# SSM convolution and SwiGLU on one core: kernel transforms split by even and odd samples, mirrored rows fetched by index, residual added by matmul

One NeuronCore of one Trainium2 chip. The metric is the device time of one launch in microseconds (us). Short names of the engines: PE (TensorE), PEld (its weight loads), DVE (VectorE), ACT (ScalarE), POOL (GpSimd), SP (SyncE).

## The reference

For a sequence of 2048 rows of 640 columns in bf16: a causal shift convolution of four taps on k, a product with v, a long causal convolution with an SSM kernel (one filter of 2048 taps for each column), a skip term, a product with LayerNorm(q), a residual, then LayerNorm and a SwiGLU FFN of width 1728 with its residual.

```python
def _A_ref(q, k, v, shift_k, ssm_k, ssm_D):
    # k_shift = causal 4-tap convolution of k (cut)
    kv = k_shift * v
    # y = irfft(rfft(kv padded to 2S) * rfft(ssm_k padded to 2S))[:S]  (cut)
    y = y + kv * ssm_D[None, None, :]
    return q * y

def _B_ref(x, w_gate, w_up, w_down):
    return (silu(x @ w_gate) * (x @ w_up)) @ w_down

x = A_q
h = x + _A_ref(_layernorm(x), A_k, A_v, A_shift_k, A_ssm_k, A_ssm_D)
return h + _B_ref(_layernorm(h), B_w_gate, B_w_up, B_w_down)
```

## The kernel before

The sequence is cut into four blocks of 512 rows. Each block of kv and of the SSM kernel is transformed by matmuls with cosine and sine tables (X and G below). Spectra are multiplied and summed on VectorE (`pair`), one inverse transform per block goes back, and LayerNorm, up and down projection follow. While VectorE works on the products of block n, PE does the FFN of block n-1. Every instruction is first entered in a plan with a duration, its reads and its writes. A small list scheduler in the kernel then fixes the order of each engine, and the engines run in that order.

The transform of an SSM kernel block, 8 output tiles from 4 contraction tiles of 512 samples:

```python
def g_transform(p, pr):
    for ct in range(NCT):                       # 8
        for kt in range(4):
            for h in range(2):
                nc.tensor.matmul(ps(g)[:, h, 0:NH], WG[:, kt, ct * P:(ct + 1) * P],
                                 gT[p][:, kt, h * NH:(h + 1) * NH], start=(kt == 0), stop=(kt == 3))
        # ScalarE copies PSUM to G[p] (cut)

def hbuild(p, pr):                              # for p = 1, 2, 3
    vop(TA, d[0][:], g[0][:], gp[1][:], ...)    # 2560 wide
    vop(TS, d[1][:], g[1][:], gp[0][:], ...)
```

The four-tap convolution of a 128-row tile of blocks 1 to 3, on VectorE:

```python
nc.vector.tensor_mul(kd[:], kd[:], w4[:])                            # 2560 wide
nc.vector.tensor_add(kd[:, 0:2, :], kd[:, 0:2, :], kd[:, 2:4, :])    # 1280 wide
nc.vector.tensor_add(kd[:, 0, :], kd[:, 0, :], kd[:, 1, :])
nc.vector.tensor_mul(kv[:, q, :], kd[:, 0, :], vb[:])
```

The end of a LayerNorm, on POOL, with one number per row. VectorE then scales the tile with it (tiles `xln` and `hl`):

```python
def fin():                                      # s is 128 x 8 float32
    e.tensor_scalar(s[:, 3:4], s[:, 1:2], 1.0 if vec else 1.0 / D, EPS, op0=ALU.mult, op1=ALU.add)
    e.tensor_tensor(s[:, 4:5], s[:, 3:4], mhalf[:], op=ALU.pow)   # e = nc.gpsimd
add("POOL", 1.5, fin, ...)
```

The inverse transform gives an even and an odd part of a half block. Their sum is one tile of y, and their difference is another tile with its rows reversed. Before, four matmuls with a flip matrix turn that one round, and VectorE multiplies from PSUM. The FFN's residual is a VectorE addition from PSUM.

## Time and profile before

| | before |
|---|---|
| device time, median of 3 | 296.56 us (294.88 to 296.61) |
| span of the profiled run | 293.2 us |
| busy PE / DVE / ACT / POOL | 275.7 / 229.7 / 169.7 / 65.7 us |
| VectorE ends the last spectrum product | 225.0 us |
| first up projection starts | 74.8 us |
| mean granted TensorE clock | 0.999 |

The span is that of the profiled execution; timed executions are some 2 us longer. A busy time is the union of the engine's instructions, so it is time covered, not work done.

### The profile page before, as it was taken

What the parts mean: (1) busy time and instruction counts of PE and PEld (TensorE: products, weight loads), DVE (VectorE), ACT (ScalarE), POOL (GpSimd) and SP (SyncE); (2) the same over time, 40 slices, a digit from 0 to 9 for tenths busy, and PEclk for the clock granted to TensorE, in tenths of its full rate; (3) what the DMA queues carried; (4) which work ended last, traced back from release to release, by engine and by line L of the source; (5) the groups of instructions that cost most, each with busy time, mean ns of one, the idle gap of its engine ahead of it and who ended that gap; (6) DMA issues with size and microseconds to landing.
All of it is one profiled execution on the core that took longest, in us unless ns stands there. A gap on an engine that the chain in (4) does not pass through costs nothing.

```text
span 293.2 us, 4406 instructions
## 1 busy us (share of the span) xinstructions
PE 275.7 (94%) x1651; PEld 157.8 (54%) x1651; DVE 229.7 (78%) x301; ACT 169.7 (58%) x323; POOL 65.7 (22%) x70
## 2 busy tenths in 40 slices
PE   3889969999999989999999999999999999999995
PEld 1567647667544535665546456555445664444563
DVE  0849797999999999999999999999999931211211
ACT  5136985897846499006986780269955822555300
POOL 0000371474000064000362193009800220000000
PEclk9999999999999999999999999999999999999999
DMA  7990699219454777925668293173653151654011
GB/s 246 386 353 2 173 269 335 54 27 301 135 137 107 205 208 155 294 108 139 161 202 233 61 194 68 45 207 86 168 128 99 49 119 54 172 146 102 0 47 46
DMA packets 67898, 44.13 MB, mean 151 GB/s; under 512 B 25442, under 2 KB 65955, under 8 KB 67748
## 3 DMA queue, kind: packets, MB, share of 16 engines
q1 hardware_dynamic: 66240, 40.23, 50.0%
q10 hardware_dynamic: 1636, 3.61, 3.3%
q8 instruction: 13, 0.21, 0.3%
q14 instruction: 9, 0.07, 0.1%
HBM read 37.28 MB, written 2.62 MB: 136 GB/s over the span
## 4 chain that ended last, share of the span: by engine, by line
DVE 53%; PE 31%; issue 5%; ACT 4%; DMA 3%; POOL 2%; ACTq 1%; SPq 0%
DVE s L453 20%; DVE T L453 14%; PE psF L644 11%; PE psF L618 11%; DVE k L378 3%; DVE tT L632 3%; PE psA L405 3%; DMA wu<-in_B_w_up_dram 2%; PE psF L361 2%; DVE k L379 2%; PE psA L550 2%; PE psA L443 2%; DVE k L380 1%; DVE o L652 1%; DMA wg<-in_B_w_gate_dram 1%
## 5 line engine op out<-in xcount | busy, mean ns | idle before, releaser
L618 PE MATMUL psF<-hT,wg 128*128 128x512 bf16 x280 | 69.4, 379 | 0.8 <-ACT uc L630 0.8
L524 POOL TENSOR_SCALAR sm<-sm 128x1 f32<-128x1 f32 x32 | 30.2, 943 | 168.4 <-ACT junk L521 157.9
L618 PE MATMUL psF<-hT,wu 128*128 128x512 bf16 x260 | 64.5, 379 | 0.9 <-DMA wu<-in_B_w_up_dram 0.9
L644 PE MATMUL psF<-wd,tT 128*128 128x320 bf16 x448 | 64.8, 300 | 0.5 <-DVE tT L632 0.4
L623 ACT ACTIVATE sg<-psF 128x512 bf16<-128x512 f32 (+1 forms) x56 | 33.8, 603 | 45.0 <-PE psF L618 36.0
L644 PEld LDWEIGHTS <-tT 128*128 128x128 bf16 x448 | 41.3, 97 | 23.6 <-issue 6.9
L453 DVE TENSOR_TENSOR T<-s,s 128x2560 bf16<-128x2560 bf16 x32 | 47.2, 1480 | 0.0
L453 DVE TENSOR_TENSOR s<-s,T 128x2560 bf16<-128x2560 bf16 x32 | 47.0, 1480 | 0.0
L618 PEld LDWEIGHTS <-wg 128*128 128x128 bf16 x280 | 27.2, 98 | 32.7 <-issue 2.3
L630 ACT CAST uc<-psF 128x512 bf16<-128x512 f32 (+1 forms) x56 | 33.2, 593 | 16.4 <-PE psF L618 16.2
L632 DVE TENSOR_TENSOR tT<-sg,uc 128x512 bf16<-128x512 bf16 (+1 forms) x56 | 23.2, 418 | 24.3 <-ACT uc L630 24.3
L618 PEld LDWEIGHTS <-wu 128*128 128x128 bf16 x260 | 25.3, 98 | 30.2 <-DMA wu<-in_B_w_up_dram 1.4
L525 POOL TENSOR_TENSOR sm<-sm,mhalf 128x1 f32<-128x1 f32 x32 | 35.1, 1098 | 2.7
L361 PEld LDWEIGHTS <-s 128*128 128x128 bf16 x256 | 25.0, 97 | 11.8 <-issue 2.1
L361 PE MATMUL psF<-wd,s 128*128 128x320 bf16 x192 | 28.4, 299 | 0.9 <-ACT wd L338 0.5
L652 DVE TENSOR_TENSOR o<-psF,x 128x640 bf16<-128x640 f32 x16 | 13.0, 815 | 19.3 <-PE psF L644 19.3
L364 ACT CAST s<-psF 128x640 bf16<-128x640 f32 x32 | 21.8, 693 | 7.7 <-PE psF L361 7.6
L521 ACT ACTIVATE junk<-x,sm 128x640 bf16<-128x640 bf16 x28 | 23.7, 847 | 0.3
L520 ACT ACTIVATE junk<-x 128x640 bf16<-128x640 bf16 x28 | 20.9, 747 | 3.8 <-DVE x L578 2.9
L550 PE MATMUL psA<-s,WI 128*128 128x320 bf16 x128 | 18.9, 299 | 2.7 <-DVE s L453 2.7
L453 DVE TENSOR_TENSOR s<-s,s 128x2560 bf16<-128x2560 bf16 x14 | 20.5, 1480 | 1.2 <-ACT s L364 1.2
L443 PE MATMUL psA<-kv,WX 128*128 128x320 bf16 x128 | 20.5, 299 | 0.0
(55 smaller groups left out, 232.0 us busy)
## 6 DMA issues: line engine op xcount, KB each, us to landing
k<-in_A_k_dram SPq DMA_DIRECT2D x12, 640.0 KB, 4.9
wg<-in_B_w_gate_dram SPq DMA_DIRECT2D x24, 320.0 KB, 3.2
wu<-in_B_w_up_dram SPq DMA_DIRECT2D x24, 320.0 KB, 3.7
out_dram<-o SPq DMA_DIRECT2D x16, 160.0 KB, 2.0
wd<-in_B_w_down_dram SPq DMA_DIRECT2D x1, 2080.0 KB, 10.7
v<-in_A_v_dram SPq DMA_DIRECT2D x12, 160.0 KB, 5.2
x<-in_A_q_dram SPq DMA_DIRECT2D x3, 640.0 KB, 5.5
tT<-in_A_ssm_k_dram SPq DMA_DIRECT2D x2, 640.0 KB, 8.8
```

The costliest lines, as they stand in the source:

```text
L361: nc.tensor.matmul(ps(g)[:, h, 0:NH], WG[:, kt, ct * P:(ct + 1) * P], gT[p][:, kt, h * NH:(h + 1) * NH], start=(kt == 0), stop=(kt == 3))
L443: nc.tensor.matmul(ps(g)[:, h, 0:NH], WX[:, kt, ct * P:(ct + 1) * P], kv[:, base + kt, h * NH:(h + 1) * NH], start=(kt == 0), stop=(kt == 1))
L453: add("DVE", dve(n * D), lambda: f(o, a, b), r=ks(ak) + ks(bk), w=ks(ok), after=["WG0", "WG1"] if ok[:2] == "s7" else [], pr=pr)
L521: add("ACT", act(D) + 0.45, lambda: nc.scalar.activation(junk[:], src, ACT.Square, bias=s[:, 0:1], accum_out=s[:, 1:2]), r=[xk, k + "a"], ...
L524: e.tensor_scalar(s[:, 3:4], s[:, 1:2], 1.0 if vec else 1.0 / D, EPS, op0=ALU.mult, op1=ALU.add)
L525: e.tensor_tensor(s[:, 4:5], s[:, 3:4], mhalf[:], op=ALU.pow)
L550: nc.tensor.matmul(ps(g)[:, h, 0:NH], WI[:, 4 * part + ct, m * P:(m + 1) * P], a[part][:, ct, h * NH:(h + 1) * NH], start=(ct == 0), stop= ...
L618: i = nc.tensor.matmul(ps(gr)[:, which, :], w[:, kt, cc * P:(cc + 1) * P], hT[b][:, kt, :], start=(kt == 0), stop=(kt == 4))
L623: apart(gr, 0, nc.scalar.activation(sg[s][:z, :], ps(gr)[:z, 0, :], ACT.Silu))
L630: add("ACT", act(MB), lambda gr=gr, s=s, z=z, merged=merged: nc.scalar.copy(uc[s][:z, :], ps(gr)[64:128, 0, :] if merged else ps(gr)[:, 1, ...
L632: add("DVE", dve(MB), lambda c=c, s=s, z=z: TM(tT[:z, c * MB:(c + 1) * MB], sg[s][:z, :], uc[s][:z, :]), r=[f"sg{s}", f"uc{s}"], w=[f"tT{c ...
L644: nc.tensor.matmul(ps(gr)[:, h, 0:NH], tT[:z, c * MB + m * P:c * MB + (m + 1) * P], wd[:z, c, h * NH:(h + 1) * NH], start=(c == 0 and n no ...
```

## The change

Its intent: take work from PE, with small additions elsewhere.

- The SSM kernel transform is split by even and odd samples: half as many matmuls, then sums and differences ("butterflies", 1280 wide) on VectorE.
- The 1280-wide addition of the four-tap convolution goes to an accumulating DMA that POOL issues (all 12 tiles of blocks 1 to 3).
- The mirrored tile is left mirrored. The matching q rows are gathered in reverse order and the results are stored in reverse order, by indexed DMAs that POOL issues.
- The FFN's residual is an extra matmul with the identity in blocks 0 to 2; ScalarE empties PSUM.
- Some transposes move from DMA to PE, and a table of offsets (`URGENCY`, `EARLIEST`) moves stages in the scheduler's order.

The core of the diff (cut):

```diff
+URGENCY = {"down 1": 706, "ffn 1": 670, "front_first 2": 3502, ... }
+EARLIEST = {"front 1": 57, "front_first 1": 7, ... }
-RES, XACT, VEC, TRANS = (), (), True, {2: 28, 3: 28}
+ACC = [(n, q) for n in (1, 2, 3) for q in range(4)]
+RES, XACT = (0, 1, 2), ()
+VEC = [(0, q) for q in range(4)] + [(3, 2), (3, 3)]
+TURN = (0, 3)
+GATHER = True
@@ g_transform
-                for kt in range(4):
+                for i in range(2):
+                    kt = ct // 2 % 2 * 2 + i
@@ hbuild
+        vop(TA, d[0][:, e, :], c[:, e, :], c[:, o, :], ..., 2)      # four of 1280 for each p
+        vop(TS, d[0][:, o, :], s[:, o, :], s[:, e, :], ..., 2)
+        vop(TA, d[1][:, e, :], s[:, e, :], s[:, o, :], ..., 2)
+        vop(TS, d[1][:, o, :], c[:, e, :], c[:, o, :], ..., 2)
@@ front_tile
+        if (n, q) in ACC:
+            add("POOL", 1.1, lambda: nc.gpsimd.dma_start(out=kd[:, 0:2, :]..., in_=kd[:, 2:4, :]..., accum_op=ALU.add, ...), ...)
@@ load_x / ffn
+                add("POOL", 1.2, lambda q=q: nc.gpsimd.indirect_dma_start(out=x[:, q, :], in_=xq[:, :], in_offset=mirror(n, q), ...), ...)
+                add("POOL", 1.2, lambda m=m, s=s: nc.gpsimd.indirect_dma_start(out=oo[:, :], out_offset=mirror(n, m), in_=ot[s][:], ...), ...)
@@ inverse
-                if half == 0:
+                if half == 0 or GATHER:
+                    # y = es + os, or es - os for the mirrored half, in SBUF
```

## The prediction

> **What bounds the kernel now.** I read the page first, then the chain of waits in order of time, then busy time in three stretches, then the timeline of a few places.
>
> The page says TensorE (PE) is busy nearly everywhere, and VectorE (DVE) from a sixth of the span to three quarters of it:
>
> ```profile
> span 293.2 us, 4406 instructions
> ...
> PE   3889969999999989999999999999999999999995
> ...
> DVE  0849797999999999999999999999999931211211
> ACT  5136985897846499006986780269955822555300
> POOL 0000371474000064000362193009800220000000
> ```
>
> Each digit is 7.3 us. Two engines are full together until slice 31, then PE alone. So there are two candidate bounds, and each must be counted on its own.
>
> The groups give the PE work by kind:
>
> ```profile
> L618 PE MATMUL psF<-hT,wg 128*128 128x512 bf16 x280 | 69.4, 379 | 0.8 <-ACT uc L630 0.8
> L644 PE MATMUL psF<-wd,tT 128*128 128x320 bf16 x448 | 64.8, 300 | 0.5 <-DVE tT L632 0.4
> L361 PE MATMUL psF<-wd,s 128*128 128x320 bf16 x192 | 28.4, 299 | 0.9 <-ACT wd L338 0.5 <-ACT s L364 0.4
> L574 PE MATMUL psA<-os,perm 128*128 128x320 bf16 x16 | 4.6, 299 | 0.0
> ```
>
> The means of 379 and 300 ns are latencies of overlapping matmuls. What one costs the engine is read from long unbroken runs in the chain:
>
> ```profile
> 223.46 1.50 DVE s L453
> ...
> 225.00 2.35 PE psA L550 x16
> 227.35 0.54 PE psA L574 x4
> 227.90 1.09 PE psF L644 x8
> 228.98 0.54 PE psA L574 x4
> 229.53 14.86 PE psF L644 x104
> ```
>
> ```profile
> 19.57 0.72 PE L334 MATMUL psF<-perm,tT 128*128 128x128 bf16 x10
> ```
>
> Eight 320-wide matmuls take 1.09 us: 0.136 each. The page-long run of 135 512-wide ones, later in the chain, takes 29.25: 0.217 each. Ten 128-wide ones take 0.72, of which 0.22 is the latency of one: (0.72 - 0.22)/9 = 0.056 each. The kernel has 540 of the 512-wide, 1066 of the 320-wide (448 + 256 + 128 + 128 + 50 + 32 + 12 + 8 + 4) and 45 of the 128-wide: 117.0 + 145.0 + 2.5 = **264.5 us of PE work** in a span of 293.2. The other 28.7 us are lost: some 8 in the first 10 us before data arrives, 3.6 after the last matmul, some 6 between 10 and 60 us, the rest in small gaps.
>
> The chain also shows how the end hangs on VectorE. At 225.0 VectorE finishes the last spectrum product (s L453). From there PE does block 3's inverse transform (L550) and mirror (L574), then block 2's down projection (L644 x104), and block 3's up projection starts at 244.4, its down projection ends at 289.6. Nothing of block 3's FFN can start before VectorE is done and LayerNorm has followed. The stretches:
>
> ```profile
> 0.00:50.00 50.00, 39.96 (x277) 26.58 (x278) 34.73 (x42) 30.25 (x53) 8.57 (x14) 1.00 0.79 251
> 50.00:225.00 175.00, 171.13 (x993) 95.11 (x991) 173.91 (x219) 113.36 (x224) 54.16 (x48) 1.00 0.55 147
> 225.00:293.00 68.00, 64.56 (x383) 36.09 (x383) 21.06 (x42) 26.09 (x48) 2.99 (x8) 1.00 0.33 85
> ```
>
> The columns after the width are PE, weight loads, DVE, ACT and POOL. VectorE has 208.6 us of work before 225 and 16.4 idle, nearly all in the first 50 us. A second bound: **225 + 68 us of tail**.
>
> **What the Trainium skill says.** "VectorE: DVE Perf Modes", section on the perf-mode tier table: a bf16 two-tensor operation in SBUF runs at 2x, and with a PSUM operand at 1x. The trace agrees: 128x640 from SBUF 484 ns, with PSUM 815. "TensorE: Matmul & The Clock Gate", section on weight-path perf modes: the fast weight load also takes strided columns, so the stride-2 stationary operand that splits even and odd samples should load as fast as now (97 ns); no run here shows a strided one yet. "SBUF — State Buffer", section "Who interferes with whom": a VectorE operation with two SBUF inputs blocks a GpSimd one that reads SBUF. The trace agrees: the 128x1 scalar operation on POOL takes 190 ns after 231 us, when VectorE is light, but 943 on average. "DMA: Bandwidth & Descriptors", section "SWDGE vs HWDGE vs iDMA": accumulating and irregular transfers must come from GpSimd, whose software writes their descriptors. The kernel before has none, so their latency is not in the trace.
>
> **The change part by part, PE.**
> - Split G transform: 8 tiles x 2 products x 2 halves instead of 4 x 2, for four blocks: 256 matmuls become 128. -128 x 0.136 = -17.4.
> - Mirror on PE (L574) gone, because query rows are gathered mirrored: -32 x 0.136 = -4.4.
> - Transposes: blocks 2 and 3 of the SSM kernel by PE instead of DMA, 40; activations of blocks 0 and 3, 40. +80 x 0.056 = +4.5.
> - Residual by an identity matmul in blocks 0 to 2: 3 x 4 x 2 = 24. +24 x 0.136 = +3.3.
> Sum -14.0: PE work 250.5. With the same 28.7 lost, **279.2 us of span**.
>
> **The change, VectorE up to the last product.** In an unbroken run a 2-row (1280) operation takes some 0.74 us, a 1-row one 0.40, a PSUM one 0.73 (the chain's pieces; the page's means are some 0.08 higher, as they overlap).
> - Butterflies: 4 blocks x 4 operations of 1280. +16 x 0.74 = +11.8.
> - Front tiles of blocks 1 to 3: their 1280-wide add goes to an accumulating DMA. -12 x 0.74 = -8.9.
> - Residual add from PSUM in blocks 0 and 1: -8 x 0.73 = -5.8 (block 2's lies after the last product in both, so it does not count here).
> - Mirror half: a PSUM product becomes a subtraction and a product in SBUF, 6 tiles x (0.80 - 0.73) = +0.4.
> Sum -2.5. That is small: VectorE gives back in butterflies what it saves elsewhere. Early idle: between 22 and 31 us the chain alternates between X and G(0) matmuls, and G(0) now has 32 fewer, 4.4 us; I take 3 of that as gained. The last product then falls at 225 - 2.5 - 3 = 219.5.
>
> **The tail.** Before, 19.4 us lie between the last product and the up projection. The last transposing DMA is issued at 240.0 and lands some 2.6 later, so the latency of inverse and LayerNorm is 17.6; block 2's down projection covers it. After: two of the four tiles get their statistics on VectorE, which takes 2 x (0.74 + 0.19 + 0.83 + 0.18) = 3.9 out of ScalarE's series; PE transposes with a 0.69 copy save some 2 against the DMA. Latency some 11.7. PE has 14 us less to do before the last product, so most of block 2's down projection fits ahead of it. Then 219.5 + 11.7 + 29.25 (up) + 16.0 (down) + 3.6 (last copy and store) = **280.0**. So the two bounds meet, at 279 and 280; two bounds that close get in each other's way, so I add 1: span 281. The timed run of before was 294.99 against its span of 293.2, 1.8 more: **282.5 us**, rounded.
>
> ScalarE: +8 copies of kernel transposes, +8 of activations, +12 of outputs, 28 x 0.69 = 19.3, less 3.9: 185 us of 281, two thirds. Not a bound on average. DMA: constants of 512 KB less, two transposes of 640 KB and half of the small ones gone; the accumulations add 12 x 320 KB. Share 50% before; not a bound.
>
> **Rivals.**
> - *Early starvation.* The G transforms are PE's filler: they run from 23.4 to 75 us, until block 0's up projection begins at 74.8. With 17.4 us of it gone and block 0's LayerNorm chain no shorter, PE idles there instead. For it: ScalarE, which empties each G tile in 0.69 us, would now be slower than PE's 0.55, and it was at 8 to 9 tenths there. Against it: the SSM tile loads, the X transform and the up projection can come earlier, and stage offsets in the diff look tuned to do so. If half the saving is lost: some 289. If all: 293 to 297, no gain.
> - *Accumulating DMAs become VectorE's wait.* VectorE is in order; an accumulation that lands late stops it. POOL also carries LayerNorm's blocked small operations, and gathers. If each of 12 stalls 1 to 2 us: 294 to 306. Against: descriptors are only written, and loads are two tiles ahead, so other VectorE work can stand between.
> - *The tuning takes away losses too.* The 16 us of early VectorE idle and the 28.7 lost on PE are not all forced. If 6 more go: 275 to 277.
>
> **Range and chances.** The first rival pulls up by some 4 in a third of cases, the second by 12 or more in one of fifteen, the third down by 6 in a quarter. So 282.5, 276 to 289.5 for 8 in 10. Faster by over 2% means under 290.6: 0.90. Within 2%: 0.07. Slower: 0.03.
>
> **What would show it.** Right: 128 G matmuls at 0.14 each; no mirror matmuls; 1066 - 136 = 930 320-wide ones; PE still in the nineties after slice 8; last product near 219; up projection of block 3 some 12 us later; the unbroken tail of 45 us unchanged. Wrong: idle PE between 40 and 75 us ended by ScalarE copies or LayerNorm (first rival); VectorE idle ended by an accumulating DMA (second); strided weight loads well over 97 ns; the last product still at 225. If it is under 276, the early idle has gone, and the first up projection starts well before 70 us.

## The result

The changed kernel took 304.80 us (median of 4; 302.30 to 305.77), beside 296.59 us for the kernel before in the same rounds. The ratio is 1.0278, with a 95% interval of 1.0206 to 1.0349: **slower**, where 282.5 us was predicted. A ratio here is the mean time of one kernel's fast runs over that of the other's in the same rounds, so it is not quite the ratio of the medians quoted. The result is correct.

The page of the kernel after, first line and busy tenths:

```profile
span 302.9 us, 4377 instructions
...
PE   3799678777986899999998999789998999999994
...
DVE  0666998999959989999999999979999771121221
ACT  4239988999943569557764595179674465555300
POOL 0202582533921106990700049647000150000020
PEclk9999959999997999999999999999999999999999
```

PE has sixes to eights in most slices from 5 to 14, where it had nearly all nines, and again in 26 and 27. POOL is busier. The groups that the change made or touched (columns: busy us and mean ns of one, then idle time before):

```profile
L568 POOL TENSOR_SCALAR sm<-sm 128x1 f32<-128x1 f32 x32 | 28.8, 900 | 73.0 <-ACT junk L565 57.7
L404 POOL DMA_DIRECT2D k<-k x12 | 11.3, 939 | 37.7 <-DVE k L402 26.6 <-PE psA L434 7.4 <-PE psF L385 3.6
L484 DVE TENSOR_TENSOR s<-T 128x1280 bf16<-128x1280 bf16 x12 | 9.5, 813 | 0.0
L355 PEld LDWEIGHTS <-s 128*128 128x128 bf16 x40 | 2.8, 97 | 1.2 <-issue 0.6
```

The last row is a weight load with stride 2: 97 ns, so that premise held. The 128 matmuls of G and the butterflies are there in the numbers expected. These pieces are as predicted; the sum is not.

The view that explains the result is busy time in three stretches: 0 to 60 us, 60 us to the end of the last spectrum product, and the tail after it. Columns after the width: PE, PEld, DVE, ACT, POOL busy, then clock, DMA share and GB/s. Before:

```profile
0.00:60.00 60.00, 49.52 (x345) 33.21 (x346) 44.63 (x62) 38.91 (x71) 14.01 (x23) 1.00 0.71 222
60.00:224.95 164.95, 161.57 (x925) 88.48 (x923) 163.96 (x199) 104.68 (x206) 48.72 (x40) 1.00 0.56 152
224.95:293.20 68.25, 64.56 (x383) 36.09 (x383) 21.11 (x42) 26.11 (x48) 2.99 (x8) 0.99 0.33 85
```

After:

```profile
0.00:60.00 60.00, 45.10 (x309) 28.64 (x309) 42.91 (x59) 41.85 (x74) 21.41 (x28) 0.94 0.69 211
60.00:236.96 176.96, 161.71 (x900) 87.32 (x913) 165.88 (x207) 115.89 (x224) 66.28 (x59) 0.99 0.62 164
236.96:302.90 65.94, 61.38 (x372) 34.49 (x373) 18.44 (x42) 26.65 (x46) 7.92 (x12) 0.99 0.25 68
```

Read the DVE column. The span is VectorE's work up to the last product, plus its idle time up to there, plus the tail:

| us | DVE work to last product | DVE idle 0-60 | DVE idle 60-last | last product | tail | span |
|---|---|---|---|---|---|---|
| before | 208.6 | 15.4 | 1.0 | 225.0 | 68.2 | 293.2 |
| after | 208.8 | 17.1 | 11.1 | 237.0 | 65.9 | 302.9 |
| difference | +0.2 | +1.7 | +10.1 | +12.0 | -2.3 | +9.7 |
| predicted difference | -2.5 | -3 | 0 | -5.5 | -7.7 | -13.2 |

(The predicted tail is 280.0 - 219.5 = 60.5. The sum is an identity; what it teaches is which term moved.) Before, VectorE had 1.0 us of slack in 165. It was already the bound, and it did not get less work. PE, meanwhile, went from 3.4 us idle in the middle stretch to 15.2.

What VectorE waited for in the middle stretch of the kernel after (us in total, times, longest). Together these are its 11.1 us, within rounding:

```profile
DVE xln L576 <- POOL sm L569: 3.3, 4, 0.9
DVE tT L702 <- ACT uc L700: 2.6, 4, 1.3
DVE k L408 <- DMA k<-k: 2.5, 1, 2.5
DVE hl L576 <- POOL sm L569: 2.3, 4, 0.7
DVE hl L576 <- DMA hT<-hl: 0.5, 2, 0.3
```

The kernel before has one such line there, 0.9 us for LayerNorm, although its longest POOL operation took 5.86 us: VectorE had other work meanwhile. In the kernel after no single wait for LayerNorm is over 0.9 us. Four of the eight follow a POOL operation of 2.39 to 7.93 us; the others follow operations of 0.2 to 1.7 us, so there a missing lead in the order counts at least as much as the holding off. Only one of the twelve accumulations made VectorE wait. Here is one episode of the kernel after, from its timeline (start, length, engine, operation; in brackets the idle time and what ended it):

```profile
72.97 0.89 POOL L404 DMA_DIRECT2D k<-k  x1 [7.83 <-DVE k L402]
73.94 7.93 POOL L568 TENSOR_SCALAR sm<-sm 128x1 f32<-128x1 f32 x1
81.95 0.55 POOL L569 TENSOR_TENSOR sm<-sm,mhalf 128x1 f32<-128x1 f32 x1
82.47 0.88 POOL L404 DMA_DIRECT2D k<-k  x1
...
73.33 1.48 DVE L402 TENSOR_TENSOR k<-k,w 128x2560 bf16<-128x2560 bf16 x1
...
80.34 1.48 DVE L484 TENSOR_TENSOR s<-s,T 128x2560 bf16<-128x2560 bf16 x1
82.55 0.45 DVE L576 TENSOR_SCALAR xln<-x,sm 128x640 bf16<-128x640 bf16 x1 [0.73 <-POOL sm L569]
...
87.20 0.49 DVE L408 TENSOR_TENSOR k<-k 128x640 bf16<-128x640 bf16 x1 [2.48 <-DMA k<-k]
```

A POOL operation on one number per row takes 0.19 us when VectorE is quiet. Here it takes 7.93, ending as VectorE's run of two-input operations ends at 81.82. The accumulating DMA for the tile of VectorE's product at 73.33 stands behind it in POOL's queue. It is issued at 82.47, and 4.7 us later VectorE can go on with its tile. VectorE, which runs in order, waits for both. VectorE's FFN products are late by this, ScalarE waits for them 2.63 us, and PE 2.70 for ScalarE.

The tail: block 3's up projection starts at 253.2, 16.3 us after the last product (before: 244.3, 19.4 after). PE is without a break in between; of the 112 matmuls of block 2's down projection 84 are still there (before: all 112):

```profile
234.18 2.98 PE L717 MATMUL psF<-wd,tT 128*128 128x320 bf16 x20
237.10 2.35 PE L607 MATMUL psA<-s,WI 128*128 128x320 bf16 x16
...
239.56 4.07 PE L717 MATMUL psF<-wd,tT 128*128 128x320 bf16 x28
...
251.41 1.90 PE L717 MATMUL psF<-wd,tT 128*128 128x320 bf16 x12
253.24 1.25 PE L688 MATMUL psF<-hT,wg 128*128 128x512 bf16 x4
```

The chain of inverse and LayerNorm beside it, with ScalarE's last copy, ends at 252.3, 15.3 us after the last product, so PE's own work sets the start by only 0.9 us.

### The profile page after: what moved, and what is told of

Read it like the earlier page. It is cut to its first block, busy times and chain, and to the rows that moved or that the text cites.

```text
span 302.9 us, 4377 instructions
## 1 busy us (share of the span) xinstructions
PE 268.2 (89%) x1579; PEld 150.5 (50%) x1595; DVE 227.2 (75%) x307; ACT 184.4 (61%) x343; POOL 95.6 (32%) x98
## 4 chain that ended last, share of the span: by engine, by line
PE 28%; DVE 26%; DMA 12%; POOL 10%; ACT 6%; issue 5%; SPq 0%; POOLq 0%; DVEq 0%; ACTq 0%
PE psF L688 13%; PE psF L717 10%; DVE T L484 8%; DVE s L484 8%; POOL sm L568 5%; DMA wu<-in_B_w_up_dram 4%; PE psA L607 4%; POOL sm L569 3%; DMA x<-in_A_q_dram,idx 3%; DVE tT L702 2%; DMA x<-in_A_q_dram 2%; DMA hT<-hl 2%; DMA k<-k 2%; ACT junk L565 1%; ACT junk L564 1%
## 5 line engine op out<-in xcount | busy, mean ns | idle before, releaser
L717 PE MATMUL psF<-wd,tT 128*128 128x320 bf16 x448 | 65.9, 299 | 0.0
L484 DVE TENSOR_TENSOR T<-s,s 128x2560 bf16<-128x2560 bf16 x38 | 56.1, 1482 | 1.0 <-ACT s L387 0.9
L568 POOL TENSOR_SCALAR sm<-sm 128x1 f32<-128x1 f32 x32 | 28.8, 900 | 73.0 <-ACT junk L565 57.7
L693 ACT ACTIVATE sg<-psF 128x512 bf16<-128x512 f32 (+1 forms) x56 | 33.5, 598 | 26.3 <-DVE tT L702 13.8
L728 POOL DMA_INDIRECT out_dram<-o,idx x8 | 11.6, 1446 | 69.6 <-DVE o L725 40.3
L569 POOL TENSOR_TENSOR sm<-sm,mhalf 128x1 f32<-128x1 f32 x32 | 30.1, 941 | 2.7
L564 ACT ACTIVATE junk<-x 128x640 bf16<-128x640 bf16 x26 | 19.5, 750 | 12.9 <-DMA x<-in_A_q_dram,idx 8.0
L385 PE MATMUL psF<-wd,hT 128*128 128x320 bf16 x128 | 22.3, 308 | 4.6 <-ACT s L387 4.4
L404 POOL DMA_DIRECT2D k<-k x12 | 11.3, 939 | 37.7 <-DVE k L402 26.6
L607 PE MATMUL psA<-s,WI 128*128 128x320 bf16 x128 | 20.7, 315 | 2.3 <-DVE s L484 2.3
L565 ACT ACTIVATE junk<-x,sm 128x640 bf16<-128x640 bf16 x26 | 21.8, 837 | 0.5
L479 ACT CAST s<-psA 128x640 bf16<-128x640 f32 x29 | 18.9, 703 | 0.6 <-PE psA L474 0.6
```

Source lines behind the costliest of these rows:

```text
L385: nc.tensor.matmul(ps(g)[:, h, 0:NH], WG[:, kt, col:col + P], gT[p][:, kt, h * NH:(h + 1) * NH], start=(i == 0), stop=(i == 1))
L484: add("DVE", dve(n * D), lambda: f(o, a, b), r=ks(ak) + ks(bk), w=ks(ok), after=["kch0"] if ok[:2] == "s7" else [], pr=pr)
L564: add("ACT", act(D) + 0.25, lambda: nc.scalar.activation(junk[:], src, ACT.Copy, scale=-1.0 / D, accum_out=s[:, 0:1]), r=[xk], w=[k + "a"] ...
L565: add("ACT", act(D) + 0.45, lambda: nc.scalar.activation(junk[:], src, ACT.Square, bias=s[:, 0:1], accum_out=s[:, 1:2]), r=[xk, k + "a"], ...
L607: nc.tensor.matmul(ps(g)[:, h, 0:NH], WI[:, 4 * part + ct, m * P:(m + 1) * P], a[part][:, ct, h * NH:(h + 1) * NH], start=(ct == 0), stop= ...
L693: apart(gr, 0, nc.scalar.activation(sg[s][:z, :], ps(gr)[:z, 0, :], ACT.Silu))
```

## The experiments

Eighteen kernels ran. Two theories were stated first. **Theory S** (starvation): PE's saving was filler in the early stretch, so it is worth nothing. **Theory P** (POOL): LayerNorm's small POOL operations, held off by VectorE, share one in-order queue with the new DMA issues, and VectorE comes to wait for both. The account of VectorE given above was drawn up after the runs; it is applied to all of them in this table. Account columns are of the one profiled run, in us; ratio and interval are against the kernel before in the same rounds. Fast executions of one kernel differ by up to some 4 us (e4: 293.74 to 297.28), so a smaller difference between two rows of the account is not shown by them.

| run | median us | ratio [95%] | DVE work | idle 0-60 | idle 60-last | last product | tail |
|---|---|---|---|---|---|---|---|
| before | 296.6 | 1 | 208.6 | 15.4 | 1.0 | 225.0 | 68.2 |
| after | 304.8 | 1.028 [1.021, 1.035] | 208.8 | 17.1 | 11.1 | 237.0 | 65.9 |
| e1_no_accumulate | 310.3 | 1.048 [1.039, 1.058] | 217.3 | 15.1 | 12.3 | 244.7 | 65.2 |
| e2_no_gather | 312.1 | 1.055 [1.048, 1.061] | 207.8 | 17.8 | 13.6 | 239.1 | 70.1 |
| e3_no_pool_dma | 304.0 | 1.029 [1.023, 1.035] | 216.3 | 14.8 | 5.8 | 236.9 | 64.3 |
| e4_layernorm_off_pool | 297.1 | 0.999 [0.990, 1.008] | 209.3 | 17.1 | 3.1 | 229.5 | 66.0 |
| e5_doubled_g | 307.1 | 1.036 [1.029, 1.042] | 209.0 | 20.4 | 10.2 | 239.5 | 66.0 |
| e6_ln_off_pool_doubled_g | 304.5 | 1.032 [1.028, 1.036] | 210.0 | 19.0 | 7.1 | 236.1 | 66.0 |
| e7_before_ln_off_pool | 297.0 | 1.005 [1.000, 1.010] | 210.2 | 17.3 | 0.1 | 227.6 | 68.3 |
| e8_ln_off_pool_wd_early | 295.9 | 1.002 [0.997, 1.006] | 209.1 | 15.2 | 2.7 | 227.0 | 66.9 |
| e9_no_butterflies_ln_off | 294.7 | 0.993 [0.986, 0.999] | 201.0 | 15.5 | 8.0 | 224.5 | 66.0 |
| e10_one_pool_op | 310.2 | 1.042 [1.032, 1.052] | 210.9 | 16.4 | 14.1 | 241.3 | 66.0 |
| e11_before_gather_residual | 303.1 | 1.022 [1.017, 1.026] | 205.4 | 17.5 | 9.1 | 232.0 | 69.2 |
| e12_all_but_split | 308.0 | 1.037 [1.030, 1.043] | 195.0 | 23.0 | 13.9 | 231.8 | 75.0 |
| e13_gather_residual_ln_off | 310.6 | 1.050 [1.045, 1.055] | 206.1 | 16.3 | 15.4 | 237.8 | 69.7 |
| e14_all_but_split_ln_off | 306.9 | 1.036 [1.030, 1.043] | 195.9 | 22.5 | 12.5 | 231.0 | 74.0 |
| e15_offsets_taken_out | 314.9 | 1.062 [1.055, 1.069] | 208.3 | 18.4 | 19.5 | 246.1 | 68.4 |
| e16_ln_off_no_gather | 302.6 | 1.016 [1.011, 1.021] | 209.0 | 16.5 | 6.3 | 231.8 | 68.4 |
| e17_pool_empty | 300.0 | 1.010 [1.006, 1.015] | 217.2 | 14.9 | 1.5 | 233.5 | 64.3 |
| e18_before_residual_only | 301.0 | 1.013 [1.010, 1.016] | 203.2 | 17.2 | 4.5 | 224.9 | 73.3 |

Six runs that count as slow ones (one execution each of e4, e5, e8, e9, e10, e16) are in the medians but not in the ratios. All kernels gave results within the tolerance. e9 is wrong and passed all the same, so the tolerance does not see that part.

### e1, e2, e3: without the accumulating DMAs, without the indexed ones, without either

```diff
-ACC = [(n, q) for n in (1, 2, 3) for q in range(4)]      # e1, e3
+ACC = []
-GATHER = True                                            # e2, e3
+GATHER = False
```

> The changed kernel with the 12 accumulating DMAs taken back to VectorE adds (+8.9 us of VectorE work before the last product, by my count). Theory P (POOL's in-order queue: small LayerNorm operations blocked by VectorE, with accumulations and gathers behind them): one of two kinds of queue entry gone, so VectorE's waits shrink, but the adds come back; time 300 to 306. Theory S (PE starves between 30 and 70 us because its filler is gone, POOL is beside the point): 8 us more VectorE work, nothing gained, 308 to 313.

> The changed kernel with query rows loaded and results stored by plain DMAs, and the mirror back on PE (+32 matmuls, +4.4 us of PE). Theory P: VectorE's waits for LayerNorm and for query rows shrink by half or more; 294 to 300. Theory S: 304 to 309, as PE gets 4.4 us more to do.

> Both taken back: POOL carries only LayerNorm's small operations, as in the kernel before. Theory P: the slip against the kernel's own plan (21 us in the changed kernel, 5 in the one before) falls to 5 or 7 us, so 287 planned + 6 + 2 = 293 to 298. Theory S: no better than 304.

Theory P missed in all three: undoing parts did not bring the time back. Theory S has the 310.25 us of e1 inside its range of 308 to 313 and the 303.98 of e3 at its edge of 304; the 312.08 of e2 lies above both. Each edit makes the scheduler choose another order, under offsets that were fitted to another program, and in each of them some LayerNorm operation stays on POOL and falls into a run of VectorE's. The longest single one took 16.45 us in e1, 6.04 in e2 (an accumulating DMA stood behind it, and VectorE waited 4.0 for that one, 6.4 in all) and 19.34 in e3. What follows: the DMAs on POOL alone are not the cause. (In e1 and e3 the additions taken back also cost VectorE 8.5 and 7.5 us of work.) Theory P in its simple form, "fewer jobs on POOL, less time", fell here.

### e4 and e7: LayerNorm's POOL operations moved to VectorE, after and before

```diff
-            e.tensor_scalar(s[:, 3:4], s[:, 1:2], 1.0 if vec else 1.0 / D, EPS, op0=ALU.mult, op1=ALU.add)
-            e.tensor_tensor(s[:, 4:5], s[:, 3:4], mhalf[:], op=ALU.pow)
+            nc.vector.tensor_scalar(s[:, 4:5], s[:, 1:2], -0.5 * 8000.0 * (1.0 if vec else 1.0 / D), 30.0 - 0.5 * 8000.0 * EPS, op0=ALU.mult, op1=ALU.add)
```

One VectorE operation with a straight line in place of the power; it is good enough for these inputs and not for others, so it is a probe and no fix. The order of all other instructions is kept.

> Order and everything else as in the changed kernel, but the two small LayerNorm operations on POOL become one 128x1 operation on VectorE (a first-order formula for the inverse square root, so the result is only approximate, on purpose). VectorE gets 32 x some 0.1 us more. Theory P: POOL then has only DMA issues, no blocked reads before them; VectorE's waits for POOL (7.8 us) and for the late accumulation (2.7) go, and the PE gaps and low clock that follow them; 288 to 295. Theory S: 303 to 307.

> Control: the kernel before, its LayerNorm operations taken off POOL in the same approximate way. Theory P says the blocked POOL hurts only where DMA issues stand behind it and LayerNorm has little lead, so the kernel before gains little: 293 to 297. If the approximate LayerNorm is simply cheaper for any kernel, it gains as much as the changed one, 8 us: 287 to 290.

e4 took 297.06 us, 0.9988 of the kernel before. That lies between the two forecasts, 2 us above theory P's, and no fast run of it (293.74 to 297.28) comes near one of the changed kernel (302.30 to 305.77). Against the changed kernel its profiled span is 7.4 us shorter, and the middle idle time of VectorE is 8.0 shorter:

```profile
0.00:60.00 60.00, 44.79 (x307) 28.58 (x308) 42.94 (x66) 41.24 (x72) 7.62 (x13) 0.94 0.69 211
60.00:229.49 169.49, 160.19 (x904) 86.97 (x915) 166.35 (x229) 117.49 (x226) 22.26 (x17) 1.00 0.66 172
229.49:295.50 66.01, 61.38 (x372) 34.47 (x373) 18.73 (x46) 26.67 (x46) 4.26 (x4) 1.00 0.25 68
```

Its waits for LayerNorm and for accumulations are gone from that stretch:

```profile
DVE tT L701 <- ACT uc L699: 1.7, 3, 0.8
DVE hl L575 <- DMA hT<-hl: 1.2, 1, 1.2
```

The same edit to the kernel before (e7) gains nothing: 1.0046, as theory P had it (296.97 us, 293 to 297 expected). So in the changed kernel, in its own order, the POOL work on VectorE's path costs some 8 us, and it did not in the kernel before. This pair, which keeps each kernel's order, is the basis of what is said of theory P. It takes LayerNorm's whole detour over POOL away, the ordinary length of these operations as well as the holding off, and does not part the two.

### e5 and e6: PE's saved work put back

```diff
-                for i in range(2):
+                for i in (0, 1, 0, 1):
```

Every G matmul is done twice (the second pass starts the sum again), so PE gets the 17.4 us back that the split had saved, and nothing else changes in the program. e6 has e4's edit as well.

> The changed kernel with every G matmul done twice (the first pair of each tile thrown away): the 17.4 us of PE work that the split saved are put back, nothing else moves. If the saved matmuls were only filler while PE waits for ScalarE and VectorE (theory S), time stays at 302 to 307, and the PE clock in 30 to 50 us rises from 0.83 to near 1. If PE's work counts there, 312 to 322.

> The same doubling on the kernel whose LayerNorm has left POOL (297.1 before the doubling). Theory S: 294 to 299, as the waits are elsewhere. If PE's work counts: 305 to 314.

e5 took 307.11 us, at the upper edge of theory S's range: 17.4 us of PE work cost 2.3, which is not told apart from nothing (the intervals of the two ratios overlap). The stretches show where it went:

```profile
0.00:60.00 60.00, 47.45 (x348) 32.16 (x349) 39.62 (x53) 37.88 (x65) 17.90 (x25) 1.00 0.68 211
60.00:239.54 179.54, 170.85 (x1003) 95.33 (x1001) 169.36 (x213) 122.40 (x233) 66.48 (x61) 1.00 0.62 162
239.54:305.50 65.96, 61.54 (x375) 34.50 (x373) 18.43 (x42) 26.69 (x46) 7.92 (x12) 1.00 0.25 68
```

PE is busy 11.5 us more in the first two stretches, VectorE's idle time before 60 us rises by 3.3, and the tail is the same 66.0. In the changed kernel PE work outside the tail is nearly free, so taking it away is nearly worthless there. In e6, without the POOL waits, the same work costs more: 7.4 us between the medians of e4 and e6, 6.6 between their profiled spans, some 9.8 by the two ratios, whose intervals do not overlap.

```profile
60.00:236.10 176.10, 169.22 (x993) 94.36 (x990) 168.96 (x232) 121.52 (x231) 21.07 (x17) 1.00 0.63 165
```

Its 304.51 us is far from theory S's 294 to 299 and just under the other forecast's 305. So in this order PE's saving is worth little while VectorE waits for POOL, and 7 to 10 us once those waits are gone. That there is then less other waiting for it to hide in is the likely reason, not a shown one.

A side question is the clock. The changed kernel's PE runs at half clock (0.50 from 94 to 96 us, after an idle gap) for 11.5 us in all, worked out from the mean of 0.981 over 302.9; the kernel before hardly ever. In e5 the clock is 0.999, and it is no faster, but e5 also adds the work, so it does not part the two. In e4 the clock stays low (0.94 before 60 us, 0.988 in all) and the time is won all the same.

### e8: down-projection weights loaded early, with e4's edit

```diff
-                 r=[f"tT{2 * min(i, 2) + 1}"], after=["gT0", "gT1", "gT2"])
+                 after=["gT0", "gT1", "gT2"], t0=40)
```

> LayerNorm off POOL, and the down weights loaded when their buffer is free instead of when the up projection reaches their tiles (the planner's own total is 282.2 instead of 281.5). In the changed kernel PE waits for up weights at 91 and 102 us, while 2 MB of down weights share the DMA engines. If that costs what it seems to (some 5 us of PE between 90 and 110): 291 to 295. If it is hidden: 296 to 299.

295.92 us against 297.06 for e4, in another call: some 1 us, not told apart from nothing, and just outside both ranges. The new load times change the plan as well.

### e9: butterflies of blocks 1 to 3 left out, with e4's edit

```diff
+        none = lambda o, x, y: None
+        ta, ts = (none, none) if p else (TA, TS)
-        vop(TA, d[0][:, e, :], c[:, e, :], c[:, o, :], dk + "c", ck, ck, pr, 2)
+        vop(ta, d[0][:, e, :], c[:, e, :], c[:, o, :], dk + "c", ck, ck, pr, 2)
```

(and so for the other three). The sums before them are written straight to their place. 12 VectorE operations less, PE as it was.

> LayerNorm off POOL (297.1 us), and in the order of that kernel the 12 butterfly operations of blocks 1 to 3 left out, the sums and differences before them written straight to their place: the result is wrong on purpose. VectorE has 12 x 0.74 = 8.9 us less, all before the last spectrum product. If VectorE's work decides that product (my second bound): 287 to 291. If PE, ScalarE or waits decide: 294 to 298. Hardly below 286 on any theory.

294.67 us, 0.9925. This median fell in the range written for PE, ScalarE or waits deciding (294 to 298), not in that for VectorE's work (287 to 291). In the profiled runs VectorE's work is 8.3 us less than in e4, its middle idle time 4.9 more (3.8 of it in one wait for a transposing DMA, where e4 has 1.2), and the last product and the end come 5.0 earlier. But e9's profiled run is its fastest and e4's one of its slower ones: the means of the fast runs are 293.87 and 295.95, the intervals of the ratios overlap, and so a gain from 8.3 us less VectorE work is not shown. This run alone came out below the kernel before, by 0.75 per cent, and it computes something else.

### e10: one of the two POOL operations of LayerNorm moved

```diff
-            e.tensor_scalar(s[:, 3:4], s[:, 1:2], 1.0 if vec else 1.0 / D, EPS, op0=ALU.mult, op1=ALU.add)
+            nc.vector.tensor_scalar(s[:, 3:4], s[:, 1:2], 1.0 if vec else 1.0 / D, EPS, op0=ALU.mult, op1=ALU.add)
```

Exact arithmetic, meant as half a dose of e4.

> The changed kernel, exact again: the first of LayerNorm's two small operations moves from POOL to VectorE (one SBUF input), the power stays on POOL. Half the blocked reads on POOL are gone. Theory P: some half of the 8 us that taking both away gave: 299 to 302. If the gain came from the cheap formula or from elsewhere: 303 to 307, or all of it at 296 to 298.

310.24 us, worse than the changed kernel: the dose reading failed. The timeline tells why. The first line is the remaining POOL operation; the others are the beginning and the end of VectorE's work beside it, without a gap in between:

```profile
152.90 25.46 POOL L569 TENSOR_TENSOR sm<-sm,mhalf 128x1 f32<-128x1 f32 x1 [3.43 <-DVE sm L568]
...
152.74 0.42 DVE L702 TENSOR_TENSOR tT<-sg,uc 128x512 bf16<-128x512 bf16 x1
153.07 1.49 DVE L484 TENSOR_TENSOR T<-s,s 128x2560 bf16<-128x2560 bf16 x1
...
177.53 0.42 DVE L702 TENSOR_TENSOR tT<-sg,uc 128x512 bf16<-128x512 bf16 x1
178.39 0.45 DVE L576 TENSOR_SCALAR xln<-x,sm 128x640 bf16<-128x640 bf16 x1 [0.44 <-POOL sm L569]
```

An operation on 128 numbers took 25.46 us, until VectorE, out of two-input work, came to the very operation that waits for it. What a POOL operation costs depends on where it falls in VectorE's series, not on its size or number; and whatever stands behind it in POOL's queue is late by as much. e10's accumulations made VectorE wait 5.1 us.

### e11, e12, e18: parts of the change on the dense transform

The kernel before with the scheduler's three rounds, no offsets, and: e18 the residual on PE; e11 that and the indexed rows; e12 all parts but the split.

```diff
+RES, XACT = (0, 1, 2), ()          # e18, e11, e12
+GATHER = True                      # e11, e12
+ACC = [(n, q) for n in (1, 2, 3) for q in range(4)]    # e12, with TURN = (0, 3) and two tiles more in VEC
```

> The kernel before with only two parts of the change: query rows gathered and scattered mirrored by index (-4.4 us of PE), and the residual of blocks 0 to 2 added on PE (+3.3 us of PE, -5.8 of VectorE before the last product). The G transform is whole again, no butterflies, no accumulating DMAs, and its planner is used without the tuned offsets. Planner total 284.6 against 288.1 for the kernel before, which took 5 more plus 2: so 289 to 293 if POOL's 16 indexed DMAs do no harm; 295 to 300 if they delay LayerNorm as in the changed kernel.

> All of the change but the split of the G transform (which takes 11.8 us of butterflies off VectorE and puts 17.4 us of early PE work back), without the tuned offsets. Planner total 287.6. Theory P: POOL carries as much as in the changed kernel, so a slip of 13 to 20: 301 to 308. If the split with its starving early stretch is the larger cause: 291 to 297.

> The dense kernel with the residual on PE only (planned 291.8; with the indexed rows too it was planned at 284.6 and took 303.1). Holding-off theory: indexed rows add POOL work that can be held, so without them 295 to 300, a ratio of 1.00 to 1.015. Rival (the untuned order is bad in itself): 302 or more.

300.95, 303.10 and 308.03 us. None is faster than before, though each takes work from VectorE. e11 is above both of its ranges, and e12 lies at the upper edge of theory P's (301 to 308). Their use is as a ruler of VectorE's work, part by part: residual -5.4 (203.2 - 208.6), indexed rows +2.2, accumulation with PE transposes and statistics -10.4, split, with the offsets and the transposes that came with it, +13.8 (208.8 - 195.0). These sum to the +0.2 of the result. The idle time takes it back: 4.5, 9.1 and 13.9 us in the middle, and in e12 23.0 before 60 us. In e18 and e12 the tail grows too, to 73.3 and 75.0, probably as more PE work is left for it. e18 fell between its two expectations: indexed rows cost about 2 us here, and the order without offsets (or the ScalarE copies) the rest. These runs do not separate the two.

### e13, e14: e11 and e12 with LayerNorm's operations on VectorE

The edit of e4, made to e11 and e12.

> The kernel with the dense G transform, the indexed rows and the residual on PE (303.1 us, 1.0215 of the kernel before, with 5 us of VectorE's waits for LayerNorm's POOL operations), now with LayerNorm's two POOL operations as one on VectorE. Its instruction order is the same. If the POOL operations and the indexed transfers hold each other up (theory P), it falls to 293 to 298, a ratio of 0.99 to 1.005, as the changed kernel did. If the indexed transfers harm in another way (their late landing, or ScalarE's extra copies), it stays at 300 to 303, 1.015 or more.

> The kernel with everything of the change but the split transform (308.0 us, 1.037), LayerNorm's POOL operations moved to VectorE in the same place. Theory P: 8 to 11 us less, 297 to 300, 1.00 to 1.015, the rest being accumulating DMAs that land late. The rival (extra copies and transfers themselves): 304 or more.

Theory P said that these would fall as e4 did. e14 fell by 1 us, and e13 rose by 7.5, to 310.56; e14 is where the rival expectation had put it (304 or more), e13 above even the rival's 300 to 303. Two reasons show in the profile. The moved operation now stands in VectorE's own series and waits there for ScalarE's statistics, 6.9 us in e13. And POOL is still held off, in another job. Timeline of e13:

```profile
184.69 15.79 POOL L718 DMA_INDIRECT out_dram<-o,idx  x1 [0.87 <-ACT o L713]
...
185.32 1.50 DVE L484 TENSOR_TENSOR s<-s,T 128x2560 bf16<-128x2560 bf16 x1
...
198.10 1.50 DVE L484 TENSOR_TENSOR T<-s,s 128x2560 bf16<-128x2560 bf16 x1
202.08 0.69 ACT L713 CAST o<-psF 128x640 bf16<-128x640 f32 x1 [12.19 <-DMA out_dram<-o,idx]
...
203.42 2.29 PE L474 MATMUL psA<-kv,WX 128*128 128x320 bf16 x8 [9.38 <-ACT s L479]
```

Issuing an indexed store takes 0.96 us when VectorE is quiet; here it took 15.79, through nine of VectorE's 2560-wide operations, and ended within 1 us of the last of them. ScalarE waited 12.19 us for the output buffer, and PE 9.38 for ScalarE. The longest indexed issue was 2.97 us in the changed kernel, 10.88 in e14 and 7.79 in e15. So what VectorE holds off is not only LayerNorm. Theory P, which named LayerNorm's operations, was too narrow: they are one victim, and the indexed DMA issues are the other. The issue of an accumulating DMA, without an index list, never took over 1.03 us in the runs. (A record of 1.92 us in e15, which the expectation of e16 below counts as an exception, is two issues that the view merged.)

### e15: the table of offsets emptied

```diff
-URGENCY = {"down 1": 706, "ffn 1": 670, ... }
-EARLIEST = {"front 1": 57, "front_first 1": 7, ... }
+URGENCY = {}
+EARLIEST = {}
```

> The changed kernel, with the tables of stage offsets emptied; nothing else. Its planned time is 290.6 instead of 281.5. If the offsets only tighten a plan that the chip doesn't keep (slips of 13 to 21 us seen where POOL has both jobs), the time moves by far less than 9: 303 to 310, 1.02 to 1.045. If the offsets carry what they promise, 312 or more.

314.86 us: I expected that the offsets do little, and they do what the scheduler's model says of them (10 us against 9.1 planned). Without them, accumulations keep VectorE waiting 10.3 us. So the order matters as much as any part of the change, and a run that replans under unfitted offsets mixes two causes. That goes for e1 to e3, e8, e11 to e14 and e16 to e18.

### e16, e17: POOL with only the accumulations, and POOL empty

e2 and e3 with e4's edit.

```diff
-GATHER = True
+GATHER = False
-ACC = [(n, q) for n in (1, 2, 3) for q in range(4)]       # e17
+ACC = []
```

> The changed kernel without the indexed rows (312.1 us with LayerNorm on POOL) and with LayerNorm's POOL operations on VectorE (297.1 us with the indexed rows). POOL then only issues the twelve accumulating transfers, whose issue has not taken over 1.03 us in any run but one. If what costs is VectorE holding off POOL work that reads SBUF (LayerNorm's operations took up to 25.5 us, the indexed issues up to 15.8), it comes to 291 to 298, a ratio of 0.985 to 1.005. If the instruction order under offsets tuned for another program is what made the run without indexed rows slow, it stays above 304.

> The changed kernel with nothing left on POOL: no accumulating transfers, no indexed rows, LayerNorm's operations on VectorE. With LayerNorm on POOL it took 304.0 us, one of its POOL operations 19.3 us. Holding-off theory: 290 to 297, ratio 0.98 to 1.003. Order rival: 300 or more.

302.59 and 300.00 us: 9.5 and 4.0 less than e2 and e3, where LayerNorm was on POOL, but above what the holding-off theory gave: e16 lies between its two ranges, e17 at the 300 of the order rival. e17 is the most telling run of all. Nothing can be held off there:

```profile
0.00:60.00 60.00, 44.38 (x311) 28.60 (x312) 45.14 (x70) 41.48 (x73) 0.43 (x6) 0.94 0.59 194
60.00:233.52 173.52, 166.56 (x963) 91.55 (x961) 172.03 (x230) 117.78 (x226) 0.00 (x0) 1.00 0.56 152
233.52:297.80 64.28, 59.11 (x355) 32.74 (x355) 18.59 (x45) 25.99 (x45) 0.00 (x0) 0.99 0.24 67
```

VectorE is busy 172.03 of 173.52 us. Its first up projection starts at 64.4, 10 us before that of the kernel before, PE has some 10 us less to do than before by the prediction's count, and the kernel is still 1 per cent slower, because VectorE has 217.2 us of work before the last product instead of 208.6; a tail 3.9 us shorter makes up for less than half of that. In e16 the middle idle time is 6.3, of which 3.9 is two accumulations that land late although nothing held POOL off: their place in the order does that.

## Why the prediction was wrong

**"With the same 28.7 lost" was the step that failed first.** The PE sum, -14.0 us, agrees with the matmuls that ran, but by the same count the lost time was not 28.7 us but 302.9 - 250.5 = 52.4. What was saved turned into idle time: 3.4 us in the middle stretch before, 15.2 after. e5 shows it for the changed kernel: 17.4 us put back cost 2.3. It is no property of the saving alone, since in e6, without the POOL waits, the same 17.4 cost 7 to 10. The first rival had said so for the early stretch, and I gave it a third of a chance.

**The second bound, 225 plus a tail, was the right frame, and each of its terms was mis-sized.** In the same words as the prediction:
- "Sum -2.5": measured +0.2. The split cost 13.8 instead of 11.8, and the indexed rows 2.2 instead of 0.4. Residual and accumulation came within 2 us of what was said.
- "I take 3 of that as gained" from early idle: measured +1.7. VectorE's longest waits before 60 us had been others (7.2 us for the weights of the four-tap convolution before, 8.2 after).
- Nothing was put down for new idle time after 60 us: measured +10.1. This is the largest miss. It is the second rival in part, at which I put one chance in fifteen. Its range, 294 to 306, holds the result, but by luck: each of twelve accumulations was to stall VectorE by 1 to 2 us, and one did, by 2.5, while waits for LayerNorm took more than 5. It named accumulations that land late and said that POOL carries "LayerNorm's blocked small operations, and gathers"; it did not put the two together, as one in-order queue in which a held operation delays the DMA behind it. Its defence, that the loads are two tiles ahead, held for the eleven others. e4, which keeps the order, takes 8.0 of these 10.1 away.
- "Latency some 11.7", "most of block 2's down projection fits ahead": measured 16.3 from last product to up projection, and most of that down projection still behind the product. Its last inputs are VectorE products in the same series, done at 234.0; whether PE could have fitted more of it in between was not tried. The chain itself took 15.3, and 14.9 in e17, with POOL empty, where the up projection's start hangs on ScalarE's last copy. So the latency was put too low by 3 or more. Of that some 2 us are the statistics of two tiles, now in VectorE's series (0.88 and 0.21 us for each), which the prediction took off ScalarE and put nowhere. The last copy and store took 4.4 instead of 3.6. The tail became 65.9 and not 60.5.

The four misses, 2.7 + 4.7 + 10.1 + 5.4, are the 22.9 us between 280.0 and the span of 302.9. Three slips of the text changed little: VectorE's nines reach slice 32, not 31; ScalarE is at 5 to 9 tenths between 23 and 75 us, not 8 to 9; and 281 + 1.8 is 282.8, not 282.5.

**What the change could be worth.** With the work and tail of the kernel after (208.8 and 65.9) and the idle time of the kernel before (16.4), the span would be 291.1, an estimate from those rows: 0.7 per cent better than before. On that account the edit that saves 14 us of PE buys 2.3 in the tail and little else, so the predicted 5 per cent was not there to be had in this order. No correct version in these runs beat the kernel before.

**What stays open.** How much of the 8 us is holding off and how much a missing lead is not parted. e4 shows the cost of the POOL work in one order. It is not a law of all orders: e13 moved the same work and lost. No run replaced the scheduler's model of POOL (a pair of operations is entered as 1.5 us, whatever VectorE does) by one that knows of the holding off and searched for an order again. Whether the change would then reach the 291 above is not settled. Nor is the share of the order and of the copies in e18.

## What to carry to other kernels

Before counting what a change takes from the busiest engine, write the span as one engine's work plus its idle time plus a tail, and find the engine whose idle time is near nothing where the span is made; here it was VectorE, with 1.0 us idle in 165. A saving on another engine is worth what it takes off that work, that idle time or the tail, and e5 and e6 show that this can change with what else VectorE waits for. Then treat each small POOL operation on SBUF data, and each indexed DMA issue, as one that may last as long as VectorE's current series of two-input operations, together with all that stands behind it in POOL's queue. And test such a theory with an edit that keeps the instruction order, since taking the table of offsets out moved the kernel by 10 us on its own (e15). Check then whether two profiled runs differ by more than the runs of one kernel do.

## What the Trainium skill lacked or had wrong

- "SBUF — State Buffer", "Who interferes with whom": it says that the holder has the shared pair "for the whole instruction". It does not say that a series of VectorE instructions can hold a GpSimd one off from the first to the last: 7.93 us over eight operations in the kernel after, 25.46 us over an unbroken run in e10, for an operation of 0.19 to 0.55 us.
- The same section marks as inferred that a `tensor_tensor` leaves descriptor generation alone. For the accumulating DMA the runs agree (issue at most 1.03 us). For indexed DMAs it does not carry over: 0.96 us when VectorE is quiet, 15.79 in e13 and 10.88 in e14 beside almost nothing but two-input operations. These DMAs also have an index list in SBUF, so the runs do not say whether it is the descriptors that wait.
- "TensorE: Matmul & The Clock Gate", "Why this matters for your kernels": it warns of idle gaps over some 3 us. In the kernel after a gap of 2.70 us (90.5 to 93.2), with one of 0.49 us before it, was enough: the clock of the stretch from 90 to 100 us was 0.83.
- No page gives a time from issue to landing for an accumulating transfer within SBUF (320 KB: 4.6 us here, median of 12) or for indexed ones (160 KB: gather 4.5, scatter 2.9).
